# Hash bits on VectorE or by Sign: half of each head's bits moved, with new planner numbers

## The chip, the cores and the metric

The kernel runs on one core of one Trainium2 chip. The metric is the device time of one execution in microseconds: the median of three runs of the kernel before is 713.45 us (713.35 to 714.23).

## What is computed

LSH attention followed by two dense blocks, all in float32. `q`, `k`, `v` are (2, 8, 768, 64), sixteen heads in all; `proj` is (64, 6).

```python
q_bits = (einsum('bhsd,dk->bhsk', q, proj) > 0)          # 6 bits for each query
k_bits = (einsum('bhsd,dk->bhsk', k, proj) > 0)          # 6 bits for each key
mask   = q_bucket[:, :, :, None] == k_bucket[:, :, None, :]
scores = where(mask, scale * q @ k.T, -1e9);  scores -= max(scores)
attn   = exp(scores);  attn /= sum(attn) + 1e-9
x      = attn @ v                                         # -> (1536, 512)
h      = max(x @ w1, x @ w2, x @ w3);  x = h @ w_out      # 512 -> 768 -> 512
g      = piecewise(x @ w_in);  out = g @ w_out2           # 512 -> 2048 -> 512
```

A query sees the keys whose six bits all equal its own.

## The kernel before, in words

**Precision.** Every float32 operand is split into a high and a low part of a shorter format, and a product is made of three matmuls (high by high, low by high, high by low). The high part is a copy that rounds, the low part a subtraction.

**Heads.** A head comes as one tile `r` of 128 partitions by 768 columns: the key's 64 features above, the query's below. `prep_scale` multiplies the query by -1/8, `prep_hi` and `prep_lo` split, and `prep_move` brings parts to other partitions, by DMAs issued on SyncE (SP) for heads 1 to 15 (`qa`, `qb`, `ql`, `kh`, `kb`), by copies of VectorE and GpSimd for head 0.

**Bits.** `bits_mm` projects both at once: three matmuls for each half of 384 columns into the bank `pj_ps`; rows 64 to 75 hold the query's twelve sums (six projections, twice), rows 96 to 107 the key's. `bits_sign` (L346) makes -1 or 1 of them on ScalarE, with a scale for each row that also undoes the query's -1/8, into `z`; `bits_rows` (L354) multiplies and adds, on GpSimd (on VectorE for head 0), which gives 0 or 1 for the query and 0 or a large number for the key, into rows 64 to 107 of `qb`. Beside the features in a matmul of 76 rows (L376) they add a large number to the negated score wherever a bit differs. `pj_ps` is one bank: the second half's matmuls wait until the first half has been read. `z` is one buffer.

**Tiles.** The attention is 96 tiles of 128 queries by 768 keys. For each: the scores (`t_qk`, four matmuls into one of two double banks `s_ps`), the smallest negated score together with a copy into `p` (`t_max`, VectorE, three buffers), the exponentials with their sums (`t_exp`, ScalarE), six transposes in two halves (`t_tr`, banks `t_ps`, one for each half), their high copies (`t_hi`, ScalarE, or VectorE where ScalarE is late) and low parts (`t_lo`, VectorE). For three tiles, a group, follow twelve matmuls with v (`g_pv`, bank `u_ps`), from one of two sets of transposed p. Each pair of heads is then divided by its sums on GpSimd (`norm_add`, `norm_mult`, `norm_hi`, `norm_lo`).

**The order.** Head 0 is written out by hand. For the rest a planner (`Work`) makes the order of each engine's queue before anything runs: each task has a cost, a due time (in tiles), what it comes after, and buffers that it takes and leaves. A task can start once its predecessors have ended, plus `HOP` where they are on another engine. Of the tasks of an engine that can start within `PATIENCE` of the first, the one with the earliest due goes next. A high copy goes to VectorE if ScalarE would be free more than `MARGIN` later than VectorE could start it. `lag` is time that a result takes after the task (a DMA's landing). The queues then run in that order; each instruction waits for its data by semaphores, whatever the planner believed. Two slices of the first dense weights are prepared inside the attention; all else of the dense layers comes behind it and is not touched.

Of the kernel before, what the change touches and what calls it, by code (L numbers as in the profile page):

```python
# [21 lines left out]
HALF = S // 2  # L22
# [19 lines left out]
class Work:  # L42

    HOP = 0.15
    MARGIN = 0.5
    PATIENCE = dict(PE=0.15, ACT=0.3, DVE=0.3, POOL=0.15, SP=0.5)

    def __init__(self):  # L50
        self.open, self.at = {}, {}
# [59 lines left out]
def lsh_attention_moe_kernel(  # L111
# [27 lines left out]
    x_hl = x_p.tile([128, 2, 4, NT], F32R, name="x_hl")  # L139
    pj_raw = const.tile([128, 108], F32, name="pj_raw")  # L140
    pj_st = const.tile([128, 2, 108], F32R, name="pj_st")
    pc_sb = const.tile([128, 3], F32, name="pc_sb")
    mhalf_sb = const.tile([128, 1], F32, name="mhalf_sb")
    half_sb = const.tile([128, 1], F32, name="half_sb")
    sc_sb = const.tile([128, 1], F32, name="sc_sb")

# [103 lines left out]
    def attention(mlp_steps):  # L250
        with ExitStack() as ax, ExitStack() as sx:
# [26 lines left out]
            def load_v(h):  # L278
                vr = v_p.tile([128, NK, D], F32, tag="vr", name="vr", bufs=1)
                nc.sync.dma_start(out=vr, in_=v[h])  # L280
                head[h]["vr"] = vr

            def pj_split():
                nc.scalar.copy(out=pj_st[:, 0, :], in_=pj_raw)
                nc.vector.tensor_tensor(out=pj_st[:, 1, :], in0=pj_raw, in1=f32(pj_st[:, 0, :]), op=ALU.subtract)
# [51 lines left out]
            def bits_mm(h, half, bank):  # L337
                hd = head[h]
                cs = slice(half * HALF, (half + 1) * HALF)
                for i, (part, name) in enumerate(((0, "hi"), (1, "hi"), (0, "lo"))):  # L340
# [2 lines left out]
                        start=(i == 0), stop=(i == 2),  # L343
                    )

            def bits_sign(h, half, bank):  # L346
                z = sm_p.tile([128, HALF], F32, tag="z", name="z", bufs=1)
                nc.scalar.activation(
                    out=z[64:108], in_=bank[64:108, 0:HALF], func=ACTF.Sign, scale=pc_sb[64:108, 2:3],
                    bias=mhalf_sb[64:108],  # L350
                )
                head[h]["z", half] = z

            def bits_rows(h, half, eng):  # L354
                z = head[h]["z", half]
                cs = slice(half * HALF, (half + 1) * HALF)
                rows = slice(64, 108)
                eng.tensor_scalar(  # L358
                    out=head[h]["qb"][rows, cs], in0=z[rows], scalar1=pc_sb[rows, 0:1],
                    scalar2=pc_sb[rows, 1:2], op0=ALU.mult, op1=ALU.add,  # L360
                )


# [155 lines left out]
            load_head(1)  # L519
            banks0 = (pj_ps, u_ps)  # L520
            halves = [slice(0, HALF), slice(HALF, S)]
            prep_hi_scaled(0, halves[0])
            prep_lo_scaled(0, 0, nc.vector)
            pj_split()
# [4 lines left out]
            prep_move(0, "qb", nc.gpsimd.tensor_copy, halves[0])  # L529
            prep_move(0, "ql", nc.vector.tensor_copy, halves[0])  # L530
            prep_move(0, "qa", nc.vector.tensor_copy, halves[0])
            bits_sign(0, 0, banks0[0])
            prep_move(0, "kh", nc.gpsimd.tensor_copy, halves[0])
            prep_move(0, "ql", nc.vector.tensor_copy, halves[1])
            bits_rows(0, 0, nc.vector)
            bits_sign(0, 1, banks0[1])
            prep_move(0, "qb", nc.gpsimd.tensor_copy, halves[1])
            prep_move(0, "kb", nc.vector.tensor_copy, halves[0])
            prep_move(0, "qa", nc.vector.tensor_copy, halves[1])
            prep_move(0, "kh", nc.gpsimd.tensor_copy, halves[1])  # L540
            bits_rows(0, 1, nc.vector)
            prep_move(0, "kb", nc.vector.tensor_copy, halves[1])

            work = Work()
# [6 lines left out]
            def place(x, users):  # L551
                return Place(raw_s[x], users)
# [8 lines left out]
            def head_tasks(h):  # L561
                due = NK * h - 9
                hp, rp = place("prep", NK), place("r", 3)
                h_place[h] = hp
                ld = None
                if h > 1:
                    ld = task("SP", 0.1, due, load_head, h, takes=[rp], lag=5)
                if h == 1:
                    hi = task("ACT", 0.75, due, prep_hi_scaled, h, after=[ld], takes=[hp], leaves=[rp])
                    lo = [task("DVE", 0.47, due, prep_lo_scaled, h, half, nc.vector, after=[hi], leaves=[rp]) for half in range(2)]  # L570
                else:
                    sc = task("POOL", 0.9, due, prep_scale, h, nc.gpsimd, after=[ld])
                    hi = task("POOL", 0.8, due, prep_hi, h, nc.gpsimd.tensor_copy, after=[sc], takes=[hp], leaves=[rp])
                    lo = [task("POOL", 1.0, due, prep_lo, h, half, nc.gpsimd, after=[hi], leaves=[rp]) for half in range(2)]
                move = {}
                for x, after in (("qa", [hi]), ("qb", [hi]), ("ql", lo)):
                    move[x] = task("SP", 0.1, due, prep_move, h, x, after=after, lag=3)
                mms, rows = [], []
                for half in range(2):
                    zp, bp = place("z", 1), place("pj", 1)  # L580
                    mms.append(task("PE", 0.52, due + 2, bits_mm, h, half, pj_ps, after=[hi] + lo, takes=[bp]))
                    sg = task("ACT", 0.69, due + 2, bits_sign, h, half, pj_ps, after=[mms[-1]], takes=[zp], leaves=[bp])
                    rows.append(task("POOL", 0.75, due + 2, bits_rows, h, half, nc.gpsimd, after=[sg, move["qb"]], leaves=[zp]))
                kh = task("SP", 0.1, due + 2, prep_move, h, "kh", after=mms + [move["ql"]], lag=3.5)
                kb = task("SP", 0.1, due + 1, prep_move, h, "kb", after=mms + rows + [move["qa"], move["qb"]], lag=2.5)
                ready[h] = [kh, kb, move["qa"], move["ql"]]
# [15 lines left out]
            def tile_tasks(n):  # L602
                h, t = divmod(n, NK)
                g, r = divmod(n, 3)
                sp, pp = place("s", 1), place("p", 2)
                tb = [place(f"t{i}", 2) for i in range(2)]
                if n % (2 * NK) == 0:
                    sums_p[h // 2] = place("sums", 1)
                if r == 0:
                    pt_p_[g] = place("pt", 4)  # L610
                qk = task("PE", 0.7, n, t_qk, n, after=ready[h], takes=[sp], leaves=[h_place[h]])
                mx = task("DVE", 0.97, n, t_max, n, after=[qk], takes=[pp], leaves=[sp])
                ex = task("ACT", 1.06, n, t_exp, n, after=[mx], takes=[sums_p[h // 2]] if n % (2 * NK) == 0 else [], lag=0.1)
                exps[n] = ex
                outs, tr = [], None
                for half in range(2):
                    tr = task("PE", 0.325, n - 4, t_tr, n, half, after=[ex, tr], takes=[tb[half]], leaves=[pp], lag=0.1)
                    hi = task("ACT", 0.38, n + 0.6, t_hi, n, half, nc.scalar.copy, after=[tr], takes=[pt_p_[g]] if r == 0 and half == 0 else [], leaves=[tb[half]])
                    work.also("DVE", 0.47, lambda a=(n, half, nc.vector.tensor_copy): t_hi(*a), hi)
                    lo = task("DVE", 0.5, n - 2, t_lo, n, half, after=[hi], leaves=[tb[half]])  # L620
                    outs += [hi, lo]
                return outs

            def group_tasks(g, outs):
                h = g // 2
                up = place("u_ps", 1)
                last = None
                for i in range(4):
                    last = task("PE", 0.52, 3 * g + 0.5, g_pv, g, 3 * i, 3, after=outs + [vready[h], last], takes=[up] if i == 0 else [], leaves=[pt_p_[g], v_place[h]])
                if g % 4 == 0:  # L630
                    u_p[h // 2] = place("u", 2)
                    uc_p[h // 2] = place("uc", 2)
                uo = place("uo", 1)
                takes = [uo] if g % 4 > 1 else [u_p[h // 2]] if g % 4 == 0 else []
                co = task("ACT", 0.38, 3 * g + 1.5, g_copy, g, after=[last], takes=takes, leaves=[up])
                adds[g] = task(
                    "SP", 0.15, 3 * g + 2.5, g_fold, g, after=[co] + ([adds[g - 2]] if g % 4 > 1 else []),
                    takes=[uc_p[h // 2]] if g % 4 == 0 else [], leaves=[uo] if g % 4 > 1 else [], lag=2.8,
                )

            def pair_tasks(p_):
# [7 lines left out]
                for half in range(2):  # L649
                    xp = place("xr", 1)  # L650
                    ad = task("POOL", 0.96, due, norm_add, p_, half, nc.gpsimd, after=[adds[4 * p_ + half], adds[4 * p_ + 2 + half]], leaves=[uc_p[p_]])
                    mu = task("POOL", 1.05, due + 3, norm_mult, p_, half, nc.gpsimd, after=[ld, ad], takes=[xp], leaves=[bb, u_p[p_]])
                    hi = task("POOL", 0.6, due + 3, norm_hi, p_, half, nc.gpsimd.tensor_copy, after=[mu])
                    task("POOL", 0.96, due + 3, norm_lo, p_, half, nc.gpsimd, after=[hi], leaves=[xp])

# [212 lines left out]
    with tc.manual_schedule():  # L868
# [1 line left out]
        nc.vector.memset(half_sb, 0.5)  # L870
        nc.vector.memset(sc_sb[0:64], 1.0)
        nc.vector.memset(sc_sb[64:128], SCALE)
        nc.vector.memset(mhalf_sb, -0.5)
        mlp_steps = mlp()
        attention(mlp_steps)
        for _ in mlp_steps:
# [42 lines left out]
```

## Time and profile before

| | |
|---|---|
| median of 3 runs | 713.45 us |
| the profiled execution | 713.44 us |
| its span, first to last instruction | 711.5 us |
| busy in the span | TensorE 698.0 us (98%), its weight loads 593.9 (83%), VectorE 521.1 (73%), ScalarE 397.3 (56%), GpSimd 316.8 (45%) |
| matmuls and weight loads | 3548 and 3548 |
| first dense matmul | 243.2 us |

The span begins with the first instruction; what lies around it makes the difference to the time. Engines are PE (TensorE's matmuls), PEld (its weight loads, which overlap matmuls), DVE (VectorE), ACT (ScalarE), POOL (GpSimd) and SP (SyncE, which issues DMAs). Ends of matmuls are modelled and stretch over the next one's start, so TensorE's busy share is no measure of how full it is.

### The profile page before, as it was taken

How to read it: one execution, taken by the hardware profiler on the slowest of the kernel's cores; microseconds unless marked ns; L12 is line 12 of the kernel's file. 1: busy time of each engine (PE TensorE's matmuls, PEld its weight loads, DVE VectorE, ACT ScalarE, POOL GpSimd, SP SyncE). 2: the span in 40 equal slices, each digit the busy share in tenths (PEclk: the TensorE clock that was granted, in tenths of full speed). 3: DMA queues.
4: the chain of work that ended last, by engine and by line, in shares of the span. 5: the costliest groups of instructions: out<-in, count | busy, mean ns of one | idle time of the engine just before them, and what ended most of it. 6: DMA issues, size and time to landing. Idle time of an engine off the chain costs nothing.

```text
span 711.5 us, 10320 instructions
## 1 busy us (share of the span) xinstructions
PE 698.0 (98%) x3548; PEld 593.9 (83%) x3548; DVE 521.1 (73%) x846; ACT 397.3 (56%) x778; POOL 316.8 (45%) x307
## 2 busy tenths in 40 slices
PE   8999999999999999999999999999999999999998
PEld 6988988898999888888888888888888888888886
DVE  6888788988888687785445256764888888888844
ACT  5998888898999633332222223666444445444430
POOL 4667757677664034343332212543443444434430
PEclk9999999999999999999999999999999999999999
DMA  5565456645442222322111112111111112211004
GB/s 162 150 158 137 131 132 174 161 112 127 117 119 54 68 91 88 105 80 76 45 46 45 53 59 89 60 59 60 59 60 60 59 60 62 80 65 61 30 0 178
DMA packets 25660, 62.80 MB, mean 88 GB/s; under 512 B 4084, under 2 KB 9812, under 8 KB 25608
## 3 DMA queue, kind: packets, MB, share of 16 engines
q1 hardware_dynamic: 25576, 62.15, 30.1%
q8 instruction: 28, 0.46, 0.3%
q14 instruction: 24, 0.20, 0.1%
q0 software_dynamic: 32, 0.00, 0.0%
HBM read 42.07 MB, written 3.19 MB: 64 GB/s over the span
## 4 chain that ended last, share of the span: by engine, by line
PE 91%; DVE 4%; ACT 3%; issue 1%; DMA 0%; DVEq 0%; ACTq 0%
PE b L712 47%; PE b L839 19%; PE u_ps L427 8%; PE t_ps L403 8%; PE s_ps L373 4%; PE s_ps L376 4%; PE pj_ps L341 2%; DVE p L383 2%; DVE pl L421 1%; ACT ph L417 1%; ACT p L395 1%; DMA r<-in_kq 0%; DVE lo L297 0%; DVE qb L358 0%; DVE qa L326 0%
## 5 line engine op out<-in xcount | busy, mean ns | idle before, releaser
L712 PE MATMUL b<-x_hl,w 128*128 128x512 f32 (+1 forms) x900 | 203.0, 382 | 0.0
L712 PEld LDWEIGHTS b<-x_hl,w 128*128 128x128 f32 x900 | 164.0, 188 | 33.7 <-POOL w L220 0.3
L739 POOL TENSOR_TENSOR g<-r,g 128x512 fp32r<-128x512 f32 x48 | 62.7, 1307 | 125.6 <-ACT g L738 125.6
L421 DVE TENSOR_TENSOR pl<-t_ps,ph 128x384 fp32r<-128x384 f32 x192 | 100.8, 553 | 19.6 <-ACT ph L417 17.8
L839 PE MATMUL b<-w,g 128*128 128x512 f32 (+1 forms) x438 | 108.4, 391 | 0.0
L220 POOL TENSOR_TENSOR w<-wg,w 128x512 fp32r<-128x512 f32 (+1 forms) x42 | 59.4, 1413 | 95.3 <-ACT w L214 79.4
L383 DVE TENSOR_SCALAR_CACHE_REDUCE p<-s_ps 128x768 f32<-128x768 f32 x96 | 91.0, 951 | 12.6 <-PE t_ps L403 10.2
L839 PEld LDWEIGHTS b<-w,g 128*128 128x128 f32 x438 | 81.8, 188 | 18.8
L193 DVE SCALAR_TENSOR_TENSOR wg<-wg,wr 128x512 f32<-128x512 f32 (+1 forms) x58 | 66.0, 1138 | 36.0 <-ACT wg L191 35.2
L395 ACT ACTIVATE p<-p,nm 128x768 f32<-128x768 f32 x96 | 90.2, 940 | 3.4 <-DVE p L383 2.6
L403 PE MATMUL t_ps<-ident,p 128*128 128x128 f32 x576 | 87.4, 274 | 4.3 <-DVE pl L421 3.5
L214 ACT CAST w<-wg 128x512 fp32r<-128x512 f32 (+1 forms) x42 | 25.4, 606 | 115.3 <-DVE wg L206 115.3
L417 ACT CAST ph<-t_ps 128x384 fp32r<-128x384 f32 x186 | 83.6, 479 | 10.8 <-PE t_ps L403 8.8
L712 PE MATMUL b<-x_hl,wx 128*128 128x512 f32 x360 | 86.1, 395 | 0.0
L403 PEld LDWEIGHTS t_ps<-ident,p 128*128 128x128 f32 x576 | 69.1, 140 | 14.5 <-DVE pl L421 6.5
L712 PEld LDWEIGHTS b<-x_hl,wx 128*128 128x128 f32 x360 | 67.8, 188 | 15.8
L373 PE MATMUL s_ps<-lo,qa 128*128 128x384 f32 x192 | 70.5, 367 | 3.2 <-DVE p L383 3.0
L819 DVE SCALAR_TENSOR_TENSOR r<-r,b 128x512 f32<-128x512 f32 x48 | 33.0, 687 | 48.2 <-ACT r L818 47.8
L376 PE MATMUL s_ps<-hi,qb 76*128 76x384 f32 x192 | 65.3, 340 | 0.5 <-DVE hi L326 0.5
L846 DVE TENSOR_TENSOR acc<-b,acc 128x512 f32<-128x512 f32 (+1 forms) x85 | 56.4, 675 | 8.0 <-PE b L839 8.0
L817 ACT ACTIVATE r<-b,half_sb 128x512 f32<-128x512 f32 x48 | 32.9, 686 | 46.2 <-PE b L712 40.8
L198 DVE TENSOR_SCALAR wg<-wg 128x512 int32<-128x512 int32 (+1 forms) x58 | 54.0, 931 | 2.7
(85 smaller groups left out, 995.5 us busy)
## 6 DMA issues: line engine op xcount, KB each, us to landing
wr<-in_w SPq DMA_DIRECT2D x50, 512.0 KB
r<-in_kq SPq DMA_DIRECT2D x15, 384.0 KB
vr<-in_v SPq DMA_DIRECT2D x16, 192.0 KB
rb<-d SPq DMA_DIRECT2D x16, 192.0 KB
wr<-in_w SPq DMA_DIRECT2D x8, 384.0 KB
qa<-hi SPq DMA_DIRECT2D x15, 192.0 KB
qb<-hi SPq DMA_DIRECT2D x15, 192.0 KB
qa<-lo SPq DMA_DIRECT2D x15, 192.0 KB
```

Of the source, the lines that this page charges most:

```text
L193: nc.vector.scalar_tensor_tensor(out=f32(g), in0=f32(g), scalar=TINY_SQ, in1=f32(high), op0=ALU.is_ge, op1=ALU.mult)
L220: nc.gpsimd.tensor_tensor(out=w[:, 1, 0:cols], in0=f32(g2), in1=f32(w[:, 0, 0:cols]), op=ALU.subtract)
L373: nc.tensor.matmul(out=o, lhsT=hd["qa"][:, qs], rhs=hd["lo"][:, ks], start=True, stop=False)
L376: nc.tensor.matmul(out=o, lhsT=hd["qb"][0:76, qs], rhs=hd["hi"][0:76, ks], start=False, stop=True)
L383: nc.vector.tensor_scalar(out=p.rearrange("p (a k) -> p a k", a=2), in0=s_ps[n % 2][:, :, 0:HALF], scalar1=MASKED, scalar2=MASKED, op0=ALU ...
L395: nc.scalar.activation(out=p, in_=p, func=ACTF.Exp, scale=-1.0, bias=tl[n]["nm"], accum_out=pair[h // 2]["sums"][:, c:c + 1],)
L403: nc.tensor.transpose(out=t_ps[half][:, j * 128:(j + 1) * 128], in_=tl[n]["p"][:, kt * 128:(kt + 1) * 128], identity=ident,)
L417: copy(out=hi, in_=src)
L421: nc.vector.tensor_tensor(out=lo, in0=src, in1=f32(hi), op=ALU.subtract)
L712: nc.tensor.matmul(out=outp, lhsT=w_[a], rhs=x_[b_], start=(i == 0 and jj == 0), stop=(i == n - 1 and jj == 2),)
L739: nc.gpsimd.tensor_tensor(out=dst[:, 1, cs], in0=src, in1=f32(dst[:, 0, cs]), op=ALU.subtract)
L839: nc.tensor.matmul(out=pb[:, cs], lhsT=gs[f][:, a, tsl], rhs=wt[:, b_, cs], start=(n == 0), stop=(n == len(terms) - 1),)
```

## The change

For heads 1 to 15 the first half's bits are compared on VectorE straight out of the bank (`bits_now`: greater than a row's edge, times 1 or the large number); the second half keeps Sign on ScalarE and one operation on GpSimd. For head 0 both halves are compared on VectorE. Six of the twelve columns of the projection that serve the query and six of those that serve the key (`c0` 64 and 96) are negated on GpSimd at the start (`pj_sign`), so that one scale serves all rows. The tile of row constants has four columns, and the constant -0.5 goes. Planner numbers change: `HOP`, `MARGIN`, patience, the cost of the scores, the lags of moves and folds, and the dues of P·V and of `norm_mult`.

```diff
-    HOP = 0.15
-    MARGIN = 0.5
-    PATIENCE = dict(PE=0.15, ACT=0.3, DVE=0.3, POOL=0.15, SP=0.5)
+    HOP = 0.2
+    MARGIN = 0.2
+    PATIENCE = dict(PE=0.1, ACT=0.3, DVE=0.3, POOL=0.5, SP=0.5)
...
+            def pj_sign():
+                for c0 in (64, 96):
+                    nc.gpsimd.tensor_scalar(
+                        out=pj_raw[:, c0:c0 + 6], in0=pj_raw[:, c0:c0 + 6], scalar1=-1.0, scalar2=0.0, op0=ALU.mult, op1=ALU.add
+                    )
...
+            def bits_now(h, half, bank):
+                rows = slice(64, 108)
+                nc.vector.tensor_scalar(
+                    out=head[h]["qb"][rows, half * HALF:(half + 1) * HALF], in0=bank[rows, 0:HALF],
+                    scalar1=pc_sb[rows, 0:1], scalar2=pc_sb[rows, 1:2], op0=ALU.is_gt, op1=ALU.mult,
+                )
...
             def bits_sign(h, half, bank):
...
-                    out=z[64:108], in_=bank[64:108, 0:HALF], func=ACTF.Sign, scale=pc_sb[64:108, 2:3],
-                    bias=mhalf_sb[64:108],
+                    out=z[64:108], in_=bank[64:108, 0:HALF], func=ACTF.Sign, scale=HUGE, bias=pc_sb[64:108, 2:3]
...
+            pj_sign()
             prep_hi_scaled(0, halves[0])
...
-            bits_sign(0, 0, banks0[0])
...
-            bits_rows(0, 0, nc.vector)
-            bits_sign(0, 1, banks0[1])
+            bits_now(0, 0, banks0[0])
...
-            bits_rows(0, 1, nc.vector)
+            bits_now(0, 1, banks0[1])
...
-                    move[x] = task("SP", 0.1, due, prep_move, h, x, after=after, lag=3)
+                    move[x] = task("SP", 0.1, due, prep_move, h, x, after=after, lag=5)
                 mms, rows = [], []
                 for half in range(2):
-                    zp, bp = place("z", 1), place("pj", 1)
+                    bp = place("pj", 1)
                     mms.append(task("PE", 0.52, due + 2, bits_mm, h, half, pj_ps, after=[hi] + lo, takes=[bp]))
-                    sg = task("ACT", 0.69, due + 2, bits_sign, h, half, pj_ps, after=[mms[-1]], takes=[zp], leaves=[bp])
-                    rows.append(task("POOL", 0.75, due + 2, bits_rows, h, half, nc.gpsimd, after=[sg, move["qb"]], leaves=[zp]))
+                    if half == 0:
+                        rows.append(task("DVE", 0.72, due + 2, bits_now, h, half, pj_ps, after=[mms[-1]], leaves=[bp]))
+                    else:
+                        zp = place("z", 1)
+                        sg = task("ACT", 0.69, due + 2, bits_sign, h, half, pj_ps, after=[mms[-1]], takes=[zp], leaves=[bp])
+                        rows.append(task("POOL", 0.75, due + 2, bits_rows, h, half, nc.gpsimd, after=[sg], leaves=[zp]))
...
-                qk = task("PE", 0.7, n, t_qk, n, after=ready[h], takes=[sp], leaves=[h_place[h]])
+                qk = task("PE", 0.75, n, t_qk, n, after=ready[h], takes=[sp], leaves=[h_place[h]])
...
-                    last = task("PE", 0.52, 3 * g + 0.5, g_pv, g, 3 * i, 3, after=outs + [vready[h], last], takes=[up] if i == 0 else [], leaves=[pt_p_[g], v_place[h]])
+                    last = task("PE", 0.52, 3 * g + 5.4, g_pv, g, 3 * i, 3, after=outs + [vready[h], last], takes=[up] if i == 0 else [], leaves=[pt_p_[g], v_place[h]])
...
-                    takes=[uc_p[h // 2]] if g % 4 == 0 else [], leaves=[uo] if g % 4 > 1 else [], lag=2.8,
+                    takes=[uc_p[h // 2]] if g % 4 == 0 else [], leaves=[uo] if g % 4 > 1 else [], lag=3.5,
...
-                    mu = task("POOL", 1.05, due + 3, norm_mult, p_, half, nc.gpsimd, after=[ld, ad], takes=[xp], leaves=[bb, u_p[p_]])
+                    mu = task("POOL", 1.05, due + 12, norm_mult, p_, half, nc.gpsimd, after=[ld, ad], takes=[xp], leaves=[bb, u_p[p_]])
...
-        nc.vector.memset(mhalf_sb, -0.5)
```

## Rows read from the trace of the kernel before

**Rows 1.** Windows: each engine's busy us (instructions) by stretch, granted clock, DMA.

```profile
core 0: us, PE busy (x) PEld busy (x) DVE busy (x) ACT busy (x) POOL busy (x), PEclk, DMA share, GB/s
17.00:233.00 216.00, 209.56 (x1356) 194.34 (x1355) 184.29 (x392) 196.77 (x428) 144.14 (x171) 1.00 0.51 130
17.00:50.00 33.00, 31.59 (x206) 29.21 (x205) 28.26 (x61) 30.57 (x67) 20.05 (x25) 1.00 0.60 148
50.00:100.00 50.00, 48.94 (x313) 44.85 (x312) 40.91 (x89) 43.66 (x95) 35.96 (x44) 1.00 0.55 142
100.00:150.00 50.00, 47.88 (x311) 44.36 (x310) 42.63 (x90) 45.66 (x99) 36.39 (x42) 1.00 0.53 143
150.00:176.00 26.00, 24.39 (x156) 22.04 (x155) 22.73 (x48) 24.21 (x53) 17.77 (x21) 1.00 0.58 145
176.00:233.00 57.00, 56.77 (x378) 53.87 (x377) 49.76 (x108) 52.66 (x117) 33.98 (x41) 1.00 0.36 90
360.00:450.00 90.00, 90.00 (x393) 73.55 (x392) 43.00 (x69) 26.94 (x48) 21.09 (x18) 1.00 0.19 61
```

**Rows 2.** Waits of TensorE, 17 to 233: us in total, times, longest.

```profile
PE t_ps L403 <- DVE pl L421: 2.8, 4, 0.8
PE s_ps L373 <- DVE p L383: 2.6, 6, 0.7
```

**Rows 3.** VectorE's groups by line, 17 to 233: busy, mean ns, idle before, releasers.

```profile
L421 DVE TENSOR_TENSOR pl<-t_ps,ph 128x384 fp32r<-128x384 f32 x183 | 96.0, 553 | 17.6 <-ACT ph L417 16.0
L383 DVE TENSOR_SCALAR_CACHE_REDUCE p<-s_ps 128x768 f32<-128x768 f32 x91 | 86.3, 951 | 12.3 <-PE t_ps L403 10.2 <-PE s_ps L376 1.5
L417 DVE CAST ph<-t_ps 128x384 fp32r<-128x384 f32 x5 | 2.8, 555 | 1.5 <-PE t_ps L403 1.3
```

**Rows 4.** The same view for ScalarE and GpSimd, 17 to 233.

```profile
L417 ACT CAST ph<-t_ps 128x384 fp32r<-128x384 f32 x178 | 79.9, 479 | 10.1 <-PE t_ps L403 8.1
L348 ACT ACTIVATE z<-pj_ps,mhalf_sb,pc_sb 44x384 f32<-44x384 f32 x28 | 18.7, 667 | 2.5 <-PE pj_ps L341 1.0 <-POOL qb L358 0.7
...
L358 POOL TENSOR_SCALAR qb<-z,pc_sb 44x384 fp32r<-44x384 f32 x29 | 19.4, 669 | 27.2 <-ACT z L348 25.3 <-DMA vr<-in_v 0.3
```

**Rows 5.** Timeline near 109: start, us, engine, line, operation [idle before, releaser].

```profile
108.11 0.82 PE L403 MATMUL t_ps<-ident,p 128*128 128x128 f32 x6
...
108.64 0.86 ACT L417 CAST ph<-t_ps 128x384 fp32r<-128x384 f32 x2 [0.28 <-PE t_ps L403]
109.15 1.02 DVE L421 TENSOR_TENSOR pl<-t_ps,ph 128x384 fp32r<-128x384 f32 x2 [0.98 <-ACT ph L417]
109.76 1.01 PE L403 MATMUL t_ps<-ident,p 128*128 128x128 f32 x6 [0.83 <-DVE pl L421]
```

**Rows 6.** The chain of waits, 17 to 243, shares by engine and line.

```profile
by line: PE u_ps L427 26.3%; PE t_ps L403 24.0%; PE s_ps L373 12.8%; PE s_ps L376 11.2%; PE pj_ps L341 5.4%; DVE p L383 4.9%; DVE pl L421 4.6%; ACT ph L417 3.7%; ACT p L395 2.7%; issue 2.5%; ACT z L348 0.6%; PE pj_ps L474 0.4%; DVE wg L206 
```

**Rows 7.** Timeline of the start, 0 to 13.

```profile
0.75 0.39 SPq L273 DMA_DIRECT2D r<-in_kq  x1
...
1.19 0.42 SPq L275 DMA_DIRECT2D pj_raw<-in_pj  x1
...
3.31 1.28 ACT L292 ACT_TABLE_LOAD   x1 [3.31 <-DMA r<-in_kq]
...
5.13 0.26 ACT L284 CAST pj_st<-pj_raw 128x108 fp32r<-128x108 f32 x1
5.26 0.94 DVE L297 SCALAR_TENSOR_TENSOR lo<-r,sc_sb,hi 128x384 fp32r<-128x384 f32 x1 [4.00 <-ACT hi L292]
...
8.19 0.66 DVE L358 TENSOR_SCALAR qb<-z,pc_sb 44x384 fp32r<-44x384 f32 x1
...
9.88 1.00 POOL L335 TENSOR_TENSOR vv<-vr,vv 128x384 fp32r<-128x384 f32 x1
10.03 1.06 DVE L358 TENSOR_SCALAR qb<-z,pc_sb 44x384 fp32r<-44x384 f32 x1
...
12.67 0.95 DVE L383 TENSOR_SCALAR_CACHE_REDUCE p<-s_ps 128x768 f32<-128x768 f32 x1
```

More of the change, by code (lines that the diff above doesn't have):

```diff
@@ L141, in lsh_attention_moe_kernel @@
     pj_st = const.tile([128, 2, 108], F32R, name="pj_st")
-    pc_sb = const.tile([128, 3], F32, name="pc_sb")
-    mhalf_sb = const.tile([128, 1], F32, name="mhalf_sb")
+    pc_sb = const.tile([128, 4], F32, name="pc_sb")
     half_sb = const.tile([128, 1], F32, name="half_sb")
@@ L355, in bits_rows @@
                 z = head[h]["z", half]
-                cs = slice(half * HALF, (half + 1) * HALF)
                 rows = slice(64, 108)
                 eng.tensor_scalar(
-                    out=head[h]["qb"][rows, cs], in0=z[rows], scalar1=pc_sb[rows, 0:1],
-                    scalar2=pc_sb[rows, 1:2], op0=ALU.mult, op1=ALU.add,
+                    out=head[h]["qb"][rows, half * HALF:(half + 1) * HALF], in0=z[rows],
+                    scalar1=pc_sb[rows, 3:4], scalar2=pc_sb[rows, 3:4], op0=ALU.mult, op1=ALU.add,
                 )
@@ L892 @@
         pj[rows, c0 + 6:c0 + 12] = proj
-    pc = np.zeros((128, 3), np.float32)
-    pc[64:70] = [0.5, 0.5, HUGE / SCALE]
-    pc[70:76] = [-0.5, 0.5, HUGE / SCALE]
-    pc[96:102] = [-0.5 * BIG, 0.5 * BIG, HUGE]
-    pc[102:108] = [0.5 * BIG, 0.5 * BIG, HUGE]
+    pc = np.zeros((128, 4), np.float32)
+    edge = np.float32(0.5 / HUGE)
+    past = -np.nextafter(edge, np.float32(1))
+    for rows, first, top in ((64, edge, 1.0), (70, past, 1.0), (96, past, BIG), (102, edge, BIG)):
+        pc[rows:rows + 6] = [first, top, -0.5 if first > 0 else 0.5, 0.5 * top]
     mw = {n: np.asarray(a) for n, a in inputs.items() if n.startswith("moe")}
```

## The prediction

> **What bounds the kernel now.** I read the stretches of the attention first (the view of windows), then the chain of waits there, then the groups of instructions by line, the waits of TensorE, and last the timeline at the start. The profiled execution took 713.44 us, of which the span is 711.5; the median of the three runs is 713.45, so the sum below, made against 713.44, stands for the median too. All of the change lies in the attention, which TensorE leaves at about 243 us for the dense layers. There a middle stretch, 360 to 450, has TensorE busy for 90.00 of 90.00 us [rows 1], with the same work before and after: I carry those 468 us over unchanged.
>
> In the attention TensorE's busy share misleads, because the ends of matmuls are modelled. The weight loads (PEld) are the better measure: there is one per matmul. In 176 to 233 they fill 53.87 of 57 us, 94.5%, and TensorE pauses hardly at all [rows 1]; I take that as what a full TensorE looks like in this mix. In 17 to 50, 50 to 100, 100 to 150 and 150 to 176 they fill 29.21, 44.85, 44.36 and 22.04 us. Divided by 0.945 and taken from the length, that leaves 2.1, 2.5, 3.1 and 2.7 us lost, or 6.3, 5.1, 6.1 and 10.3% of each stretch, 10.4 us of 159 in all. These 10.4 us are what a better balance or order can win in the steady part; the change takes no matmul away.
>
> What holds TensorE up is a loop over three engines. Its direct waits are for VectorE: 2.8 us in front of transposes, until the low part has been cut out of the transposed bank, and 2.6 us in front of the scores, until the maximum has released the scores' bank [rows 2]. VectorE itself waits 16.0 us for ScalarE's high copies before cutting, and 10.2 us before maxima for TensorE's transposes, which give back one of three buffers of p [rows 3]. ScalarE waits 8.1 us before high copies for TensorE [rows 4]. One turn stands in the timeline: transposes at 108.11, copies at 108.64, the low parts at 109.15 after VectorE had been idle for 0.98, and the next transposes at 109.76 after 0.83 idle [rows 5]. By the chain of waits in 17 to 243, VectorE carries 9.5% (4.9 and 4.6), ScalarE's copies and exponentials 6.4%, Sign 0.6%, and nearly all of the rest is TensorE [rows 6]. So Sign is hardly ever the last thing waited for; what it does is fill ScalarE, which in 17 to 233 is busy for 196.77 of 216 us, against 184.29 for VectorE and 144.14 for GpSimd [rows 1].
>
> **The change part by part.** *ScalarE and GpSimd lose.* Of each later head's two Signs one goes: 15 times 667 ns [rows 4], 10.0 us over the attention. In 17 to 176, where the lost time is, it is 11 or 12 of them, 7.7 us. ScalarE is busy there for 30.57 + 43.66 + 45.66 + 24.21 = 144.1 us, 90.6% [rows 1]; 136.4 us, 85.8%, remain. GpSimd loses 15 times 669 ns [rows 4], and gains nothing: it isn't a bound.
>
> *VectorE gains.* 15 compares of 44 partitions by 384 columns out of PSUM. The trace has no such compare. From below the nearest row is VectorE's copy of 384 columns out of PSUM at 555 ns [rows 3], from above the two scalings of the same 44 by 384 on VectorE in the start, 0.66 and 1.06 us [rows 7]. I take 555, which has the same source and length. In 17 to 176 that is 11.5 times 0.555 = 6.4 us onto 28.26 + 40.91 + 42.63 + 22.73 = 134.5 us [rows 1], so 140.9, or 88.6% against 84.6%. Behind a compare in VectorE's queue stand a maximum or a low part, for which TensorE waits. The compare itself waits for the three matmuls of bits where the planner put it too early; the upper bound is that each of 15 puts its whole length onto the path, 15 times 0.555 = 8.3 us (15.9 at 1.06).
>
> *What the shift is worth.* The stretches of before give two readings. Ordered by ScalarE's share, 87.3, 91.3, 92.6 and 93.1%, the lost shares are 5.1, 6.1, 6.3 and 10.3% [rows 1]. At 85.8% I expect no more than the 5.1% of the best of them: 159 times 5.1% is 8.1 us, 2.3 less than 10.4. Ordered by VectorE's share, 81.8, 85.3, 85.6 and 87.4%, the same losses rise as well, and at 88.6% it would be at least 10.3%, 16.4 us, 6.0 more. Both can't hold. I take the first, because VectorE's longest wait is for ScalarE (16.0 of its 31.7 idle us [rows 1, 3]): a compare that falls into such a pause costs nothing, and with ScalarE less full the pause is shorter. The last stretch, 176 to 233, has ScalarE at 92.4 and VectorE at 87.3% and loses nothing; it warns that the order of the work counts for as much as the load, and it keeps me from taking more than 2.3.
>
> *Planner's numbers.* HOP, MARGIN, the patience, the dues and the lags change no instruction by themselves, only the order in each queue and which high copies go to VectorE. A margin of 0.2 in place of 0.5 sends more of them: 5 copies were moved in 17 to 233 [rows 3]; ten more would put 5.6 us on VectorE and take ten times 479 ns [rows 4], 4.8 us, off ScalarE. The P·V matmuls, due at 3g + 5.4, may stand behind up to two or three tiles' scores; they hold one of two sets of transposed p, and ScalarE's first copy of the group after next would wait for that. The transposes keep their dues, and SP's moves are only believed to land later (5 for 3), with more than a head's length in hand. From below the orders could win all 10.4 us (which holds the 2.3), from above they could lose as much again as the worst stretch, 10.3% of 159 in place of 10.4 us, +6.0. The rows say nothing for either side, so I take 0. SP issues the same DMAs, and TensorE's clock, granted in full in every stretch (1.00) [rows 1], gives no reason to move.
>
> *The start.* VectorE works from 5.26 to the first maximum at 12.67 almost without a break [rows 7], so its sum counts. The two scalings, 0.66 and 1.06 us [rows 7], become two compares at 0.555: −0.6 at best, and none if the compare costs what the scaling did. The second scaling ran beside GpSimd's subtraction (9.88, 1.00 long [rows 7]) and ended just behind it. I take −0.5. By the Trainium skill (SBUF — State Buffer, Who interferes with whom) a VectorE scaling of SBUF data can take the port pair that it shares with GpSimd, while an instruction with at most one SBUF input outside the two-port modes does not contend; a compare out of PSUM would then lose the 0.4 us of difference for sure, which gives the same −0.5 or −0.6, and if the row's length had another reason, −0.2. Turning the projection's signs adds two small GpSimd instructions ahead of the projection's split. They are hidden: the projection is asked for at 1.19 and ScalarE splits it at 5.13, right behind its table load (3.31, 1.28 long) and its first high part [rows 7]. Two of at most 0.67 each would end by about 5.0 if the projection lands as the head's first part did, some 2.5 us after its issue. Without that cover up to 1 us would come back. The Sign's leaving ScalarE there frees it for the next head, off the path. The removed memset of one column stands on a queue that waits for the first head anyway: 0.
>
> **Sum:** 713.44 − 2.3 (steady part) − 0.5 (start) + 0 (orders, end of the attention, dense layers) = 710.6 us.
>
> **The rivals.** *Nothing comes of it* (713.4, from 712.0 to 714.9). TensorE is nearly full, keeps every matmul, and a pause that goes in one place returns at the next, as the saturated last stretch with its equally full ScalarE suggests. Against it: 10.4 us of pauses are there to be had. Beside it stands a rule of the Trainium skill (Perfetto Trace Analysis, Identifying the Most-Contended Engine): improve the engine that is fullest, and judge TensorE by its weight loads. By those it is TensorE, 90.0% in 17 to 233 against 91.1 for ScalarE and 85.3 for VectorE; the rule names the one engine from which this change takes nothing, and so speaks for no gain.
>
> *Slower: VectorE becomes the link that holds TensorE.* This is the second reading: a compare in front of a low part keeps a transposed bank shut for 0.56 us, TensorE waits, and everything behind it. Price 6.0 − 0.5 = +5.5, 718.9, at its full size; half of it gives 716. It decides once more than about a third of the compares (2.8 of 8.3 us) fall on the path. For it: TensorE's waits end on VectorE [rows 2], whose share of the chain is the larger, 9.5%; a narrower margin sends copies there too. Against: VectorE's 31.7 idle us.
>
> *Slower by the order:* P·V held back keeps ScalarE waiting for a set of transposed p; 0.2 us in each of 31 groups would be +6.2, less 2.8: 716.8.
>
> *More than forecast:* the new order fills TensorE as the last stretch did. Two thirds of the 10.4 us and the start: 713.4 − 7.4 = 706.0, or less; at most 702.5.
>
> **How the numbers follow.** About 1.4 us, 0.2%, is what a measurement can tell from no change here. Forecast (712.0 to 706.0) 0.47; more than forecast 0.09; nothing 0.17; slower by VectorE 0.17; slower by the order 0.10. So faster 0.56, same 0.17, slower 0.27. The range leaves out the 0.09 below 706.0 and about 0.10 above 716.0 (the full prices of the slower cases): 706.0 to 716.0. The forecast's own range is 706.0 to 712.0.
>
> **What would show it.** Right: 17 compares on VectorE at about 0.55 us, 15 Signs on ScalarE; the weight loads' share up from 88.3 to about 89.6% in 17 to 176, and the first dense matmul at 240.4 in place of 243.2; VectorE's wait for high copies below 16 us; the first maximum near 12.2. Wrong: TensorE's waits for VectorE (5.4 us) grow with compares in front of them (VectorE held it), ScalarE's copies waiting for P·V (the order), or no stretch gaining while ScalarE is emptier (TensorE was the bound). A compare of 0.7 us or more would break the choice of its price.

## The result, and the profile after

The changed kernel takes 706.77 us (median of 4 runs, 706.61 to 709.68) against 713.46: a ratio of 0.9916, 95% interval 0.9904 to 0.9928, or 6.0 us by the ratio and 6.7 by the medians. I had said 710.6, with a range of 706.0 to 716.0. The time lies inside that range, but my 2.8 us were less than half of what came.

The profiled execution of the changed kernel took 706.61 us, span 704.7. Its windows, with the columns of [rows 1]; the attention now ends near 236, so the whole stretch is 17 to 226 here:

```profile
core 0: us, PE busy (x) PEld busy (x) DVE busy (x) ACT busy (x) POOL busy (x), PEclk, DMA share, GB/s
17.00:226.00 209.00, 205.71 (x1355) 197.03 (x1356) 194.32 (x412) 182.71 (x409) 135.29 (x158) 1.00 0.52 135
17.00:50.00 33.00, 32.24 (x214) 30.50 (x215) 30.14 (x65) 29.71 (x68) 20.93 (x26) 1.00 0.58 152
50.00:100.00 50.00, 50.00 (x336) 48.93 (x335) 46.56 (x102) 43.97 (x99) 33.88 (x41) 1.00 0.56 144
100.00:150.00 50.00, 48.95 (x327) 47.66 (x326) 46.63 (x97) 42.43 (x95) 35.20 (x42) 1.00 0.62 164
150.00:176.00 26.00, 24.52 (x150) 21.57 (x149) 25.18 (x53) 22.35 (x50) 16.39 (x18) 1.00 0.49 135
176.00:226.00 50.00, 50.00 (x336) 48.37 (x335) 45.82 (x99) 44.25 (x101) 28.90 (x35) 1.00 0.36 84
360.00:450.00 90.00, 90.00 (x392) 73.44 (x392) 44.64 (x67) 30.48 (x55) 22.20 (x19) 1.00 0.20 65
```

The weight loads fill 97.9% of 50 to 100, where before it was 89.7 [rows 1], and 94.3% of 17 to 226. TensorE does the same work in less time, while VectorE is now the fuller of its partners (93.0%, ScalarE 87.4). The dense layers are unchanged, and the first dense matmul comes at 236.2 in place of 243.2. Of the gain 0.3 us lies in the start. The one bad stretch is 150 to 176, where the weight loads fill 83.0% (84.8 before): there VectorE is busy for 25.18 of 26 us, with parts of the two weight slices beside its own work.

VectorE's and ScalarE's groups in 17 to 226 (busy, mean ns, idle before, releasers):

```profile
L431 DVE TENSOR_TENSOR pl<-t_ps,ph 128x384 fp32r<-128x384 f32 x182 | 93.1, 551 | 11.1 <-ACT ph L427 8.2
L393 DVE TENSOR_SCALAR_CACHE_REDUCE p<-s_ps 128x768 f32<-128x768 f32 x91 | 86.1, 947 | 2.7 <-PE s_ps L386 2.4
L353 DVE TENSOR_SCALAR qb<-pj_ps,pc_sb 44x384 fp32r<-44x384 f32 x14 | 9.6, 686 | 0.5
L427 DVE CAST ph<-t_ps 128x384 fp32r<-128x384 f32 x12 | 6.6, 554 | 0.2 <-PE t_ps L413 0.2
...
L427 ACT CAST ph<-t_ps 128x384 fp32r<-128x384 f32 x170 | 74.2, 482 | 20.6 <-PE t_ps L413 20.0
L360 ACT ACTIVATE z<-pj_ps,pc_sb 44x384 f32<-44x384 f32 x14 | 8.1, 578 | 3.2 <-issue 1.4 <-PE pj_ps L346 0.9 <-POOL x_hl L517 0.6
```

The waits of TensorE in the same stretch (us, times, longest):

```profile
PE s_ps L386 <- DMA hi<-qb: 1.0, 1, 1.0
PE t_ps L413 <- ACT p L405: 1.0, 3, 0.5
PE s_ps L383 <- DVE p L393: 0.9, 3, 0.5
PE t_ps L413 <- DVE pl L431: 0.3, 1, 0.3
```

Two waits of VectorE have shrunk [rows 3]: that in front of low parts for ScalarE's copies from 16.0 to 8.2 us, and that in front of maxima for transposes from 10.2 to nothing. The idle time has gone to ScalarE, which now waits 20.0 us for transposes where it waited 8.1 [rows 4]. TensorE's own waits for VectorE have fallen from 5.4 us (2.8 and 2.6 [rows 2]) to 1.2. What is left of its direct waits is 1.0 us for a moved row (`qb`) and 1.0 for exponentials.

The start of the changed kernel, where [rows 7] had the scalings:

```profile
3.44 0.38 POOL L284 TENSOR_SCALAR pj_raw<-pj_raw 128x6 f32<-128x6 f32 x2 [1.47 <-DMA pj_raw<-in_pj]
...
5.08 0.26 ACT L289 CAST pj_st<-pj_raw 128x108 fp32r<-128x108 f32 x1
...
8.23 0.69 DVE L353 TENSOR_SCALAR qb<-pj_ps,pc_sb 44x384 fp32r<-44x384 f32 x1
...
9.83 1.00 POOL L340 TENSOR_TENSOR vv<-vr,vv 128x384 fp32r<-128x384 f32 x1
9.99 0.69 DVE L353 TENSOR_SCALAR qb<-u_ps,pc_sb 44x384 fp32r<-44x384 f32 x1
...
12.34 0.96 DVE L393 TENSOR_SCALAR_CACHE_REDUCE p<-s_ps 128x768 f32<-128x768 f32 x1
```

### The profile page after: what moved, and what is told of

The parts are those of the page before. It is cut to its first block, busy times and chain, and to the rows that moved or that the text cites. A ratio compares the mean times of both kernels' runs of the same rounds, so it can differ in the third digit from the quotient of the medians.

```text
span 704.7 us, 10307 instructions
## 1 busy us (share of the span) xinstructions
PE 694.7 (99%) x3548; PEld 596.6 (85%) x3548; DVE 531.4 (75%) x866; ACT 381.4 (54%) x755; POOL 307.7 (44%) x294
## 4 chain that ended last, share of the span: by engine, by line
PE 92%; DVE 4%; DMA 2%; ACT 1%; issue 1%; POOL 0%; DVEq 0%; ACTq 0%; POOLq 0%
PE b L725 47%; PE b L852 19%; PE u_ps L437 8%; PE t_ps L413 8%; PE s_ps L383 4%; PE s_ps L386 4%; PE pj_ps L346 2%; DVE pl L431 1%; DMA hi<-qb 1%; DVE p L393 1%; ACT ph L427 1%; DMA r<-in_kq 0%; ACT p L405 0%; DVE lo L302 0%; DVE qa L331 0%
## 5 line engine op out<-in xcount | busy, mean ns | idle before, releaser
L431 DVE TENSOR_TENSOR pl<-t_ps,ph 128x384 fp32r<-128x384 f32 x192 | 98.1, 551 | 13.3 <-ACT ph L427 10.2
L427 ACT CAST ph<-t_ps 128x384 fp32r<-128x384 f32 x180 | 78.7, 482 | 21.5 <-PE t_ps L413 20.8
L413 PE MATMUL t_ps<-ident,p 128*128 128x128 f32 x576 | 80.2, 274 | 2.0 <-DVE pl L431 1.0
L383 PE MATMUL s_ps<-lo,qa 128*128 128x384 f32 x192 | 68.5, 357 | 1.5 <-DVE p L393 1.4
```

The source lines that it names most:

```text
L383: nc.tensor.matmul(out=o, lhsT=hd["qa"][:, qs], rhs=hd["lo"][:, ks], start=True, stop=False)
L413: nc.tensor.transpose(out=t_ps[half][:, j * 128:(j + 1) * 128], in_=tl[n]["p"][:, kt * 128:(kt + 1) * 128], identity=ident,)
L427: copy(out=hi, in_=src)
L431: nc.vector.tensor_tensor(out=lo, in0=src, in1=f32(hi), op=ALU.subtract)
```

## The experiments

Times are medians; ratios are to the kernel before, measured beside each, with 95% intervals. "Bits" are the compares, the turned signs and the start; "numbers" are the planner's. "Lead" is counted in the order of TensorE's queue: the tiles, of 96, whose scores stand in it ahead of the last transposes of the tile four back. It is 17 in the kernel before and 1 in the changed one. With three buffers of p the maximum of tile n can't be written before the transposes of tile n - 3 have given a buffer back, so scores that come too early leave VectorE waiting in front of the maximum.

### Which part brings it

One run has the bits (and the start) with all of the old planner numbers, one the old bits with all of the new numbers. In short, e1's edit to the changed kernel; e2 makes the reverse one in the kernel before:

```diff
 e1_bits_only, from the changed kernel (shortened)
-    HOP = 0.2;  MARGIN = 0.2;  PATIENCE PE=0.1, POOL=0.5;  qk 0.75;  lags 5, 3.5;  due 3 * g + 5.4;  due + 12
+    HOP = 0.15; MARGIN = 0.5;  PATIENCE PE=0.15, POOL=0.15; qk 0.7;  lags 3, 2.8;  due 3 * g + 0.5;  due + 3
```

> The changed kernel with every planner number of before (HOP, MARGIN, patience, costs, lags, dues): only the compares, the projection's signs and the start are new. If the load moved off ScalarE brings the gain: 707 to 709 us. If the planner's numbers bring it: 712 to 714, of which the start gives 0.3. If VectorE suffers from the compares: above 714.

> The kernel before (both halves by Sign and GpSimd) with all of the new planner numbers. If the numbers bring the gain: 707 to 709 us. If the load moved off ScalarE brings it: 712 to 714. If the two need each other: both this run and the one with the bits alone stay above 711.

Bits alone: 713.87 us, 1.0004 (0.9994 to 1.0013). Numbers alone: 715.08, 1.0024 (1.0013 to 1.0034). Neither brings anything; together they bring 0.9916. VectorE's two groups in 17 to 226, with the bits alone (in an execution of 711.27 us, the fastest of ten) and then with the numbers alone:

```profile
L431 DVE TENSOR_TENSOR pl<-t_ps,ph 128x384 fp32r<-128x384 f32 x177 | 93.5, 553 | 11.9 <-ACT ph L427 10.7
L393 DVE TENSOR_SCALAR_CACHE_REDUCE p<-s_ps 128x768 f32<-128x768 f32 x89 | 84.4, 951 | 8.1 <-PE t_ps L413 7.4 <-PE s_ps L386 0.5
```

```profile
L421 DVE TENSOR_TENSOR pl<-t_ps,ph 128x384 fp32r<-128x384 f32 x175 | 90.9, 553 | 21.1 <-ACT ph L417 19.0
L383 DVE TENSOR_SCALAR_CACHE_REDUCE p<-s_ps 128x768 f32<-128x768 f32 x87 | 82.0, 948 | 3.6 <-PE s_ps L376 2.9 <-PE t_ps L403 0.5
```

In the same stretch of the kernel before:

```profile
DVE pl L421 <- ACT ph L417: 15.7, 26, 1.9
DVE p L383 <- PE t_ps L403: 10.2, 23, 0.9
```

So the bits bring the wait for copies down to 10.7 us and leave 7.4 of the wait for transposes; the numbers all but end the wait for transposes (0.5) and raise that for copies to 19.0.

### Is it the load on ScalarE?

In each `bits_now` of a later head a Sign of a constant is issued on ScalarE, its result unused. The queues are otherwise the changed kernel's (shortened; it writes `z`, the buffer of the second half's Sign):

```diff
+                    nc.scalar.activation(out=z[64:108], in_=ident[64:108, 0:1].to_broadcast([44, HALF]), func=ACTF.Sign, ...)
```

> The changed kernel with the Sign of each first half put back on ScalarE as a spare one of a constant (15 times about 0.58 us, its result unused), unknown to the planner: every queue keeps its order, only ScalarE's load is that of before. If the load taken off ScalarE is what lets the new order work: 711 to 715 us, VectorE waiting 15 us or more for high copies. If the order alone does it: 706.5 to 708.5.

713.14 us, 0.9995 (0.9986 to 1.0005): 15 times 610 ns on ScalarE cost the whole gain, though the order is the good one. The wait for copies is back, that for transposes stays gone:

```profile
L436 DVE TENSOR_TENSOR pl<-t_ps,ph 128x384 fp32r<-128x384 f32 x175 | 90.3, 552 | 17.4 <-ACT ph L432 15.6
L398 DVE TENSOR_SCALAR_CACHE_REDUCE p<-s_ps 128x768 f32<-128x768 f32 x88 | 83.0, 945 | 0.4
...
L359 ACT ACTIVATE z<-ident,pc_sb 44x384 f32<-44x384 f32 x14 | 8.5, 610 | 0.4
```

The spare Sign hardly waits (0.4 us idle before it), a head's two Signs together (610 and 577 ns) are no longer than those of before (667 each), and GpSimd and the start keep what the change gave them, so it is ScalarE's load that matters: with the new order the gain needs the lighter ScalarE, and e1 shows that the lighter ScalarE alone doesn't give it.

### Which number?

One number each, put into the kernel before (e3), changed in the changed kernel (e4 to e7, e11), or added to the bits alone (e12):

```diff
 e3_pv_due_only, before:  - 3 * g + 0.5   + 3 * g + 5.4        e4_pv_due_back, changed:  the reverse
 e5_hop_back:             - HOP = 0.2     + HOP = 0.15         e6_margin_back:           - MARGIN = 0.2  + MARGIN = 0.5
 e7_patience_back:        - PE=0.1        + PE=0.15            e11_hop_025:              - HOP = 0.2     + HOP = 0.25
 e12_bits_and_hop:        the bits alone, - HOP = 0.15  + HOP = 0.2
```

> The kernel before with one number changed: P.V due at 3g + 5.4 in place of 3g + 0.5. If holding P.V back behind scores is what feeds VectorE and ScalarE: 708 to 711 us, and VectorE's idle time in front of maxima (12.3 us in 17 to 233) falls below 6. If another number or the bits do it: 713 to 714.

> The changed kernel with P.V due at 3g + 0.5 again, all else new. If P.V's due carries the gain: 710 to 713 us, VectorE's idle time in front of maxima back above 8 us. If it doesn't: 706.5 to 708.

> The changed kernel with HOP back at 0.15 alone. With the bits alone at 713.9, the new numbers alone at 715.1 and both at 706.8, one of the numbers that order TensorE's queue must matter. If HOP does: 710 to 714 us, VectorE's idle time in front of maxima back above 6 us in 17 to 226. If not: 706.5 to 708.5.

> The changed kernel with MARGIN back at 0.5 alone: fewer high copies go to VectorE (12 in the changed kernel). If those copies carry the gain: 710 to 714 us, VectorE waiting longer for ScalarE's high copies. If not: 706.5 to 708.5.

> The changed kernel with TensorE's patience back at 0.15 alone. If a shorter patience (taking what can start first rather than what is due first) carries the gain: 710 to 714 us. If not: 706.5 to 708.5.

> The changed kernel with HOP at 0.25 in place of 0.2. If a longer believed handoff is better in itself (0.15 gave 719.9, 0.2 gives 706.8): 704 to 708 us. If each value only deals another order, good or bad by chance: anywhere in 705 to 720, and its time follows VectorE's two waits.

> The kernel with the bits alone and one new number, HOP at 0.2. If HOP is what the compares need: 706 to 709 us. If the numbers only work together: 711 to 716. Its time should follow VectorE's waits for transposes and for high copies in either case.

| kernel | us | ratio (interval) | lead |
|---|---|---|---|
| e2, all numbers, old bits | 715.08 | 1.0024 (1.0013 to 1.0034) | 0 |
| e3, P·V's due alone, old bits | 715.44 | 1.0034 (1.0015 to 1.0053) | 3 |
| changed kernel | 706.77 | 0.9916 (0.9904 to 0.9928) | 1 |
| e4, P·V's due back | 707.67 | 0.9926 (0.9906 to 0.9945) | 3 |
| e6, MARGIN back | 706.35 | 0.9902 (0.9887 to 0.9917) | 8 |
| e7, patience back | 709.00 | 0.9941 (0.9925 to 0.9958) | 2 |
| e12, bits and HOP 0.2 | 710.23 | 0.9961 (0.9945 to 0.9976) | 4 |
| e11, HOP 0.25 | 711.67 | 0.9984 (0.9974 to 0.9993) | 13 |
| e1, bits alone | 713.87 | 1.0004 (0.9994 to 1.0013) | 24 |
| e5, HOP back | 719.85 | 1.0099 (1.0070 to 1.0127) | 15 |

P·V's due and MARGIN, on which I had spent words, move nothing that shows when they are taken back in the changed kernel (MARGIN does with HOP at 0.15, as e17 below shows). HOP matters most, but a longer believed handoff isn't better in itself: 0.15, 0.2 and 0.25 give 719.9, 706.8 and 711.7. I read it as dealing another order. HOP at 0.2 with the bits (e12) brings 3.6 of the 7.1 us between the bits alone and the changed kernel; TensorE's patience gives 2.2 back (e7). The cost of the scores, the lags, `norm_mult`'s due and GpSimd's patience were not tried one by one. In this table the kernels with the bits fall into two groups by the lead: up to 8, 706.4 to 710.2; 13 or more, 711.7 and above. The groups are close, and single runs of e11 and e12 overlap. Within a group the lead orders nothing, and two runs below with a lead of 0 (e15, e18) take over 714. Nor do VectorE's two waits order the times, though I had expected that for e11 and e12: e15 has them as short as the changed kernel. Of the forecasts, e3 and e5 came out slower than any case that I had given, and e7 and e12 between two.

### Taking the wait away, then the order

A fourth buffer for p ends the wait for transposes without touching a queue of the attention; the planner still counts three, and a weight buffer makes the room:

```diff
-                p = p_p.tile([128, S], F32, tag="p", name="p")
+                p = p_p.tile([128, S], F32, tag="p", name="p", bufs=4)
-    WEARLY, WBUFS = 5, 7
+    WEARLY, WBUFS = 4, 7
```

> The kernel before with four buffers for p in place of three (four early weight buffers in place of five make the room); the planner still counts three, so all queues of the attention keep their order. It takes away VectorE's wait in front of maxima for transposes (10.2 us in 17 to 233) and nothing else. If two waits must both go, this one and that for ScalarE's high copies: 712 to 714 us, the wait for transposes near 0, the wait for copies 16 us or more. If this wait alone is the cost: 706 to 709.

> The kernel with the bits alone (every planner number of before), with four buffers for p and the same order of the attention's queues. If both waits must go, the compares have taken the one and the buffer takes the other: 706 to 709.5 us with none of the new numbers. If the new numbers do something else than end the wait for p's buffers: 712 to 714.5.

In the kernel before: 711.27 us, 0.9970 (0.9958 to 0.9982). With the bits alone: 711.34, 0.9972 (0.9963 to 0.9982). Both lie between the ranges that I had given; 706 to 709.5 for the second, which two separate waits would have given, missed. The buffer is worth 2.1 us in the kernel before and 2.5 with the bits. The wait for transposes is gone, but the wait for copies has taken its place: 26.3 us in the kernel before, and 16.5 with the bits alone (10.7 with three buffers). VectorE with the bits alone and four buffers:

```profile
L431 DVE TENSOR_TENSOR pl<-t_ps,ph 128x384 fp32r<-128x384 f32 x177 | 94.0, 553 | 18.2 <-ACT ph L427 16.5
L393 DVE TENSOR_SCALAR_CACHE_REDUCE p<-s_ps 128x768 f32<-128x768 f32 x88 | 82.8, 945 | 2.9 <-PE s_ps L386 2.8
```

My reading is that transposes that stand behind scores in TensorE's queue are late for ScalarE too, whatever the buffers: ScalarE waits 19.0 us for them here, 16.4 with three buffers. So the order itself had to be tried: scores of tile n behind the transposes of tile n - 4, which makes the lead 0. (`trs` keeps each tile's last transposes.)

```diff
-                qk = task("PE", 0.7, n, t_qk, n, after=ready[h], ...)
+                qk = task("PE", 0.7, n, t_qk, n, after=ready[h] + [trs.get(n - 4)], ...)
```

> The kernel with the bits alone and every planner number of before, with one more condition: the scores of tile n come in TensorE's queue behind the transposes of tile n - 4. In its queue 24 of 96 tiles' scores stood four tiles ahead of the transposes (17 in the kernel before, 1 in the changed one). If that lead is what the new numbers took away: 706 to 709.5 us, near the changed kernel, with none of its numbers. If the numbers do something else: 712 to 715.

> The kernel before with the same one condition on TensorE's queue, ScalarE's load as it was. If the order needs the lighter ScalarE: 711.5 to 715.5 us, as with the new numbers alone (715.1), VectorE waiting 15 us or more for high copies. If the order alone can do it once the lead is held: 707 to 710.

Bits alone with this line: 708.30 us, 0.9929 (0.9915 to 0.9944), 5.6 us less than without it and near the changed kernel, with none of its numbers. The kernel before with this line: 716.18, 1.0034 (1.0021 to 1.0047). So this order pays only with the lighter ScalarE, and the lighter ScalarE only with such an order. VectorE in the first of the two: the wait for transposes is down from 7.4 to 0.6 us, that for copies is where it was (10.3, 10.7 with the bits alone), and the weight loads of 17 to 226 are at 192.07 us, against 188.91 with the bits alone:

```profile
L431 DVE TENSOR_TENSOR pl<-t_ps,ph 128x384 fp32r<-128x384 f32 x180 | 94.0, 553 | 12.7 <-ACT ph L427 10.3
L393 DVE TENSOR_SCALAR_CACHE_REDUCE p<-s_ps 128x768 f32<-128x768 f32 x90 | 84.6, 948 | 5.0 <-PE s_ps L386 4.2 <-PE t_ps L413 0.6
```

### The slow order, and a faster kernel

> The changed kernel with HOP back at 0.15, which took 719.9 us with 15 tiles' scores four tiles ahead, with the same condition. If the lead is the cause there too: 706 to 710 us. If HOP's order is bad for another reason: 714 or more.

> The changed kernel with HOP back at 0.15 and the condition on scores (714.6 us), and MARGIN back at 0.5 as well. With the narrow margin 23 high copies went to VectorE, which carried 19% of the chain of waits; with 0.5 it is 3 to 5. If these copies made VectorE the link: 705 to 709 us. If HOP's order is bad for another reason: 712 to 716.

The same line in e5 (HOP at 0.15): 714.63 us, 1.0018 (1.0009 to 1.0028), 5.2 less, but short of 706 to 710. VectorE's two waits are as short as in the changed kernel (7.6 us for copies, none for transposes), and still it is 7.9 us slower. The chain of waits in 17 to 240 names VectorE's low parts, maxima and high copies for 21.4% (in 17 to 226 of the changed kernel 12 copies went there, here 23 in all):

```profile
by line: PE u_ps L437 25.1%; PE t_ps L413 20.8%; PE s_ps L383 10.2%; DVE pl L431 9.8%; PE s_ps L386 9.1%; DVE p L393 9.0%; PE pj_ps L346 4.8%; issue 3.1%; DVE ph L427 2.6%; ACT ph L427 2.3%; DVE sums L480 0.9%; ACT p L405 0.8%; ACT u L451 0
```

With MARGIN back at 0.5 as well (e17) 5 copies are left, and the time is 710.20, 0.9963 (0.9950 to 0.9976): another 4.4 us, though not the 705 to 709 that I expected. The kernel next to it, with the same line and the same MARGIN but HOP at 0.2 (e16, below), takes 704.19. So 6.0 us of HOP's order are explained neither by the lead nor by the copies; that cause stays open.

> The changed kernel with MARGIN back at 0.5 (706.4 us, 8 tiles' scores four ahead) and the same condition. If the lead costs about 0.3 us for each of such tiles: 703 to 706 us, below both kernels. If 8 or fewer cost nothing any more: 705.5 to 707.

> The kernel of 704.2 us (changed kernel, MARGIN 0.5, scores of n behind the transposes of n - 4) with the condition one tile tighter: behind the transposes of n - 3. If less lead is better still: 702 to 704 us. If VectorE now waits for scores instead (its wait in front of maxima for score matmuls, 2.5 us, grows): 705 to 712.

The changed kernel with MARGIN at 0.5 and the line is the fastest of all: 704.19 us, 0.9870 (0.9855 to 0.9885), 2.6 us below the change. No high copy goes to VectorE, and the weight loads fill 95.0% of 17 to 226:

```profile
17.00:226.00 209.00, 206.88 (x1367) 198.63 (x1367) 193.26 (x404) 187.74 (x426) 135.00 (x158) 1.00 0.51 135
```

One tile tighter, behind the transposes of n - 3, is far too tight: 715.69, 1.0038 (1.0023 to 1.0053). VectorE's wait for scores grows from 2.5 us (e16) to 8.0, ScalarE's for maxima from 0.9 to 5.6, and VectorE's for copies from 9.3 to 16.3:

```profile
ACT ph L427 <- PE t_ps L413: 19.3, 36, 1.2
DVE pl L431 <- ACT ph L427: 16.3, 27, 0.9
...
DVE p L393 <- PE s_ps L386: 8.0, 13, 1.0
...
ACT p L405 <- DVE p L393: 5.6, 11, 0.7
```

So of the bounds tried in this kernel the middle one is best: none gives 706.35, three tiles at most (two and three mixed) 704.19, two at most 715.69.

## Why the prediction was right in direction and wrong in size

- **The parts.** Right: 15 Signs gone, 17 compares, GpSimd's sign turning hidden (3.44 to 3.82, the split at 5.08), the dense layers unchanged. The compare takes 686 ns, not the 555 that I took: it lies by the scaling of the same shape, at 0.66, and not by the plain copy from PSUM. No cost of it shows: TensorE's waits for VectorE fell. The Sign that stays became cheaper, 578 ns for 667, which I had not foreseen.
- **The start.** −0.5 forecast, −0.33 measured (first maximum 12.67 to 12.34): 2 times 0.69 for 0.66 and 1.06. The second compare ran beside GpSimd's subtraction without being stretched, 0.69 us as the first. This agrees with the Trainium skill (SBUF — State Buffer, Who interferes with whom): a VectorE instruction with one SBUF input or fewer, outside the two-port modes, doesn't contend with GpSimd.
- **What the shift is worth, −2.3.** Wrong as a step. It read one effect out of the stretches, the load's, and the bits alone, with the start in them, give +0.5 us (e1, within its interval of none). With the new order the Sign's load is worth 6.4 us (e8 against the changed kernel), with the scores held back the bits are worth 7.9 (e14 against e13): the load has no price without an order. That the stretches before differ in order as well as in load, as the last one had warned, is my reading of why the step failed.
- **The orders, 0.** This is the term that failed most. "The rows say nothing for either side, so I take 0" priced the numbers by themselves, and by themselves they are worth +1.7 (e2). Their worth appears only on a ScalarE that has room: with the bits in place they bring −7.1 (713.87 to 706.77), and the whole change −6.7. A sum of terms has no place for this; −2.3, −0.5 and 0 could not be added. So the direction was right partly by luck: of the terms only the start's −0.3 is borne out by itself. A hint was there: [rows 3] showed two waits of VectorE with two releasers, 16.0 and 10.2 us, and each part shortened one of them. But the waits alone don't tell which order is good (e10, e15); what else makes one so stays open.
- **The ceiling, 10.4 us.** "I take that as what a full TensorE looks like": 94.5% of weight loads is not full. The changed kernel reaches 97.9% in 50 to 100, and so even my saturated stretch had something to give.
- **The rivals.** VectorE didn't become the link in the changed kernel. In e15 its share of the chain is 21.4%, and with the narrow margin's copies taken back (e17) 4.4 us go, though the order changes with them. P·V's due, the other slower rival, moved nothing in e4; put into the kernel before (e3) it gave +2.1, but its one run at a mean granted clock of 1.00 took 713.26. For no gain I had named a rule of the Trainium skill (Perfetto Trace Analysis, Identifying the Most-Contended Engine), optimize the engine with the highest occupancy first, and had read it as naming TensorE. My own figures name another: ScalarE 91.1%, TensorE's weight loads 90.0. So the rule names the engine that the change relieves, and speaks for a gain. The runs bear it out in part: relieving ScalarE alone gave nothing (e1), with the new order it gave the whole gain (e8).

## What to carry to other kernels

In a loop over several engines look for every wait that ends on the same engine, with its releaser: a change that shortens one of them may show little while the other stays or grows (here nothing for the bits or the numbers, 2 us for the fourth buffer), so test parts alone and together before a term is put at zero. A lighter engine pays only if the order of the queues uses it. A direct condition on the order (here: scores no more than three tiles ahead of transposes) can be tried before numbers that deal it anew: it gave 2 to 6 us in three kernels that have the bits, and no gain in the kernel before. How full an engine can be is read from the best stretch that any run reaches, not from the best of one trace.

## What the runs showed of the hardware that I had not expected

A pause of TensorE can cost twice. In the profiled execution of e5 (722.75 us) a matmul waited 2.29 us for a moved row until 124.00, and the granted clock then fell to half, from 2.4 to 1.2 GHz, until about 132. Windows of that run (granted clock third from the end):

```profile
119.00:121.00 2.00, 2.00 (x16) 1.92 (x14) 1.27 (x4) 1.84 (x6) 1.34 (x3) 1.00 0.19 57
121.00:123.00 2.00, 0.71 (x3) 0.19 (x1) 1.55 (x3) 1.16 (x3) 1.00 (x1) 1.00 0.72 205
123.00:125.00 2.00, 1.00 (x7) 0.97 (x8) 0.00 (x0) 0.00 (x0) 1.03 (x2) 1.00 0.82 216
125.00:127.00 2.00, 1.27 (x8) 1.03 (x7) 1.83 (x5) 1.78 (x4) 1.92 (x3) 0.63 0.00 0
127.00:129.00 2.00, 2.00 (x10) 1.90 (x10) 1.29 (x3) 1.17 (x3) 1.85 (x3) 0.50 0.00 0
129.00:131.00 2.00, 2.00 (x8) 2.00 (x8) 1.97 (x6) 1.45 (x3) 1.74 (x4) 0.50 0.00 0
131.00:133.00 2.00, 2.00 (x11) 1.97 (x10) 0.20 (x1) 0.23 (x1) 1.97 (x2) 0.67 0.11 18
```

Six transposes took 1.48 us at 127.64, against 0.82 at 119.24. In e10 a pause of 2.50 us for a moved row, and in e3 one of 2.12 us for a low part, were followed by stretches at half clock too. Runs of one kernel can differ with it: e5 took 718.28 and 718.40 us at a mean granted clock of 1.00, and 721.29 and 722.75 at 0.998 and 0.995. Part of e5's median of 719.85, and of e3's 715.44, is this.

And the Sign of 44 by 384 took 667 ns with a scale for each row [rows 4] but 578 with one constant scale, in both cases with a bias for each row.
